# Score slots, direct plain heads and a merged ninth block in the attention half of a one-core kernel

## The chip, the core and the metric

The kernel runs on one NeuronCore of a Trainium2 chip. The core has five engines with instruction streams of their own: PE (TensorE: matrix products), DVE (VectorE) and ACT (ScalarE: elementwise work; both read the matmul results in PSUM), POOL (GpSimd: elementwise work on SBUF, and DMA issue) and SP (DMA issue only). Each engine runs its own stream strictly in order and waits on semaphores for the others. The metric is the device time of one execution in microseconds (us), as a median of runs.

## The reference, cut to what matters

```
# q, k, v: 8 batches x 8 heads x 576 rows x 64
scores = 0.125 * q @ k.T;  mask: heads 0-3 a plain band of 32 keys back,
                                  heads 4-7 every 4th key of 128 back
attn   = softmax(masked scores);  x = heads of (attn @ v) side by side    # 8 x 576 x 512
u      = x + real(fft(fft(x, axis=1), axis=2))
un     = (u - mean(u)) / sqrt(var(u) + 1e-6)
out    = u + relu(un @ w_ch1) @ w_ch2          # 512 -> 2048 -> 512
```

`w_ch1` and `w_ch2` arrive as 64-bit floats and are narrowed on the chip.

## The kernel before

The program is built by a planner. Each piece of work is an `add(engine, cost, function, reads, writes, priority)`; `Plan.run` simulates the engines with the costs written beside the pieces and, whenever an engine is free, gives it the ready piece of lowest priority number. The order that comes out is what each engine then executes; on the chip nothing but data dependences and buffer reuse holds a piece back. The constants at the top (`P_ST`, `P_W`, `NGANG`, ...) are offsets in those priorities, so changing them moves work on all engines.

**Attention.** A batch has 4 head pairs (2 plain, 2 dilated); a pair is cut into 2 units, so there are 64 units, 8 for each batch. `attend` makes one unit: 16 score matmuls (20 in a pair's second unit, which also holds the ninth block of 64 rows) of 64x96 into two PSUM banks; on DVE, for each 128x96 block, one custom instruction that masks, scales and takes the row maximum, with a second one that reads the maximum out (L663); on ACT one exponential for each block (L669); PE transposes (L683); an ACT copy to SBUF (L685, L689); value matmuls (L696); on DVE the row sum, its reciprocal and the multiplication (L706, L708, L709, L714) into `xt` and `xl`. The buffer "sc" is both score banks together, so the scores of one unit wait until the masks of the unit before have read them. The ninth block has its two heads in different banks and takes two 64-row mask instructions.

**Store and fold.** `store` writes a pair's rows to DRAM (`xsp`, `xsm`: rows folded in a forward and a mirrored half). Batch 0's plain heads go by DMA from `xt` (lent space in `ut`) straight into the `x` tiles in SBUF. `mix` folds the tiles (L853, L855, L867 to L877), multiplies them with DFT tables along the sequence (L904, L926) and along the channels (L950, L956), and adds. The constant `NFD = 1` puts the fold of batch 0 on DVE; other batches have it on POOL. The tables come by POOL's DMA queue, chained behind a one-element copy that reads `xt` of a chosen unit (`gone`, L581, L588).

**Fill.** `fill` is the first 6 of 16 column blocks of the feed-forward (L1080 up, L1096 down) on 256 tokens, put between attention work as soon as normalised rows and narrowed weights exist. `narrow` narrows a 64-bit block with ACT's absolute value (L1023) and four DVE steps (L1025, L1028, L1031, L1034); the last one zeroes what is below the 32-bit range. The remaining 10 column blocks (L1361, L1459, L1426) follow at the end.

**Warm-up matmuls.** `start` offers PE up to 250 pairs of matmuls on a zero tile (`blank`, L558) at the worst priority: the planner puts them wherever its simulation sees PE idle, until the first fill buffer ("ff") is taken. They are in the program for good: PE executes them in order even where work is ready behind them.

## Time and profile before

| what | value |
|---|---|
| time, median of 3 runs | 1022.49 us (1022.06 to 1023.35) |
| time of the profiled execution | 1022.32 us |
| its span in the profile | 1020.5 us |
| busy share PE, DVE, ACT, POOL | 99%, 74%, 47%, 29% |

The profile covers one execution. Its 1022.32 us hold the span of 1020.5 us, from the first to the last instruction, and 1.8 us around it. A busy PE counts warm-up matmuls too. By stretches: up to about 86 us the warm-up matmuls lie between attention work; from there to 552 us attention, mixing and fills share PE; from 552 us on PE runs the remaining column blocks.

### The profile page before, as it was taken

The page shows a single profiled execution, that of the slowest core. Times are in us where ns is not written, and L with a number is a line of the kernel's source. Part 1 is how long each engine was busy: PE and PEld are TensorE (multiplying, and loading weights), DVE is VectorE, ACT ScalarE, POOL GpSimd, SP SyncE. Part 2 cuts the span into 40 slices and gives each one's busy share as a digit, 9 for nine tenths or more (in the row PEclk, how much of TensorE's full clock was granted, in tenths as well). Part 3 has the DMA queues.
Part 4 walks back from the last instruction along what each step waited for, and adds up shares of the span by engine and source line. Part 5 has one row for each costly group of instructions (what it writes and reads, how often), then busy time and mean ns, then how long its engine had stood idle before and what let it go on. Part 6 is the DMA issues. An engine that isn't in the chain of part 4 may idle for free.

```text
span 1020.5 us, 22187 instructions
## 1 busy us (share of the span) xinstructions
PE 1006.4 (99%) x8347; PEld 898.2 (88%) x8347; DVE 750.4 (74%) x2203; ACT 479.4 (47%) x1186; POOL 291.4 (29%) x348
## 2 busy tenths in 40 slices
PE   9999999999999999999999999999999999999998
PEld 8788788888888888998988899999999989898987
DVE  4799967687867677686778876858585858585846
ACT  4776754464645444342445543535252525252522
POOL 2626454436243441846132510101010101010200
PEclk9999999999999999999999999999999999999999
DMA  9978765477656434432455232323232323232211
GB/s 313 305 240 252 220 199 175 146 209 212 197 151 195 120 118 135 150 105 93 132 169 155 84 83 83 84 83 83 83 84 83 83 84 83 83 84 83 83 62 42
DMA packets 99428, 138.49 MB, mean 136 GB/s; under 512 B 9838, under 2 KB 62619, under 8 KB 99321
## 3 DMA queue, kind: packets, MB, share of 16 engines
q1 hardware_dynamic: 94368, 126.10, 41.8%
q0 software_dynamic: 4032, 9.57, 3.2%
q8 instruction: 65, 1.06, 0.4%
q10 hardware_dynamic: 920, 1.41, 0.4%
q14 instruction: 43, 0.34, 0.1%
HBM read 99.24 MB, written 37.21 MB: 134 GB/s over the span
## 4 chain that ended last, share of the span: by engine, by line
PE 84%; DVE 8%; DMA 4%; issue 1%; ACT 1%; POOL 1%; ACTq 0%; SPq 0%; DVEq 0%; POOLq 0%
PE bank L1361 24%; PE bank L1459 20%; PE bank L1096 12%; PE bank L1080 11%; PE bank L950 3%; PE bank L696 3%; PE bank L683 3%; PE bank L632 2%; PE bank L558 2%; PE bank L904 2%; DMA ut<-in_w_dram 2%; PE bank L1426 1%; DVE pm L663 1%; DVE low L1088 1%; DMA ut<-us 1%
## 5 line engine op out<-in xcount | busy, mean ns | idle before, releaser
L1361 PE MATMUL bank<-low,wb 128*128 128x512 f32 x1080 | 255.9, 389 | 0.0
L1361 PEld LDWEIGHTS bank<-low,wb 128*128 128x128 f32 x1080 | 197.9, 188 | 37.4 <-ACT xb L1367 0.5
L1080 PE MATMUL bank<-ut,low 128*128 128x256 f32 x1296 | 168.0, 283 | 0.5 <-DVE low L1088 0.4
L1080 PEld LDWEIGHTS bank<-ut,low 128*128 128x128 f32 x1296 | 157.9, 189 | 3.7 <-DVE low L1088 1.5
L1096 PE MATMUL bank<-low 128*128 128x512 f32 x648 | 155.8, 393 | 0.0
L1124 POOL DMA_INDIRECT ut<-us,flip_sb x20 | 41.3, 2064 | 371.7 <-DVE ut L1181 243.1
L1096 PEld LDWEIGHTS bank<-low 128*128 128x128 f32 x648 | 118.7, 188 | 24.5 <-DVE low L1088 0.9
L1367 ACT ACTIVATE xa<-bank 128x256 f32<-128x256 f32 x90 | 34.2, 380 | 169.8 <-PE bank L1361 169.8
L669 ACT ACTIVATE pm<-pm,mx 128x96 f32<-128x96 f32 x256 | 83.7, 370 | 55.5 <-DVE mx L663 52.3
L1398 DVE TENSOR_TENSOR y<-xa 128x384 f32<-128x384 f32 x45 | 26.1, 581 | 95.5 <-ACT xa L1367 95.2
L1203 DVE STREAM_TRANSPOSE ut<-ut 128x512 f32<-128x512 f32 (+1 forms) x76 | 71.4, 977 | 11.4 <-DMA ut<-us 8.2
L1170 DVE TENSOR_TENSOR ut<-ut,bank 128x512 f32<-128x512 f32 (+1 forms) x136 | 73.1, 547 | 2.1
L1459 PEld LDWEIGHTS bank<-w2s,low 128*128 128x128 f32 x588 | 71.7, 188 | 2.1
L1459 PE MATMUL bank<-w2s,low 128*128 128x256 f32 x588 | 72.1, 278 | 0.0
L1086 ACT ACTIVATE low<-bank 128x256 fp32r<-128x256 f32 x108 | 41.2, 382 | 65.7 <-PE bank L1080 65.3
L1088 DVE SCALAR_TENSOR_TENSOR low<-bank,low 128x256 fp32r<-128x256 f32 x108 | 45.0, 419 | 31.4 <-ACT low L1086 30.5
L663 DVE CUSTOM_DVE_ANT_0 pm<-bank,mask_sb 128x96 f32<-128x96 f32 x256 | 55.5, 247 | 11.6 <-PE bank L632 10.4
L1459 PEld LDWEIGHTS bank<-w2s,hm 128*128 128x128 f32 x483 | 58.9, 188 | 1.8
L1459 PE MATMUL bank<-w2s,hm 128*128 128x256 f32 x483 | 59.2, 278 | 0.0
L1040 ACT CAST low<-y 128x640 fp32r<-128x640 f32 (+1 forms) x50 | 35.8, 717 | 40.0 <-DVE y L1400 24.8
L1116 ACT COPY row<-bank 128x512 f32<-128x512 f32 x36 | 21.0, 585 | 66.2 <-PE bank L1096 59.2
L1459 PE MATMUL bank<-low 128*128 128x256 f32 x420 | 51.5, 278 | 0.0
(182 smaller groups left out, 1833.5 us busy)
## 6 DMA issues: line engine op xcount, KB each, us to landing
qk<-in_qk_dram SPq DMA_DIRECT2D x30, 576.0 KB
vt<-in_v_dram SPq DMA_DIRECT2D x31, 438.8 KB
us<-uc SPq DMA_DIRECT2D x36, 257.0 KB
part<-row SPq DMA_DIRECT2D x36, 256.0 KB
wst<-in_w_dram SPq DMA_DIRECT2D x18, 512.0 KB
ut<-us SPq DMA_DIRECT2D x36, 256.0 KB
ut<-part SPq DMA_DIRECT2D x36, 256.0 KB
ut<-us SPq DMA_DIRECT2D x64, 128.0 KB
```

Source lines behind the costliest of these rows:

```text
L663: nc.vector.tensor_tensor_reduce(prob(i)[ps_], sc()[e][ps_, KB * (i // 2):KB * (i // 2) + KB], mask_sb()[ps_, kind], -0.125, 3.0e38, ALU.a ...
L669: add("ACT", 0.265, lambda i=i: nc.scalar.activation(out=prob(i), in_=prob(i), func=AF.Exp, bias=mx()[:, i:i + 1], scale=-1.0), ((mx, i),) ...
L1040: add("ACT", act(n), lambda: nc.scalar.copy(out=dst(0), in_=src()), need, ((key[0], (key[1], 0)),), prio)
L1080: nc.tensor.matmul(z()[:, :n_tok], lhsT=wf()[a][:, kk], rhs=ut()[:, p, kk], start=(kk == 0 and n == 0), stop=(kk == KT - 1 and n == 2),)
L1086: add("ACT", act(n_tok) - 0.05, lambda: nc.scalar.activation(out=h()[:, 0, :n_tok], in_=z()[:, :n_tok], func=AF.Relu), (z,), ((h, 0),), prio)
L1088: add("DVE", dve(n_tok), lambda: nc.vector.scalar_tensor_tensor(h()[:, 1, :n_tok], z()[:, :n_tok], 0.0, h()[:, 0, :n_tok].bitcast(F32), op ...
L1096: nc.tensor.matmul(acc(), lhsT=h()[:, a, P * s:P * s + P], rhs=wf()[:, p], start=(first and n == 0), stop=(last and n == 2),)
L1124: add("POOL", 1.04, lambda: nc.gpsimd.indirect_dma_start(dst(), None, us[idx // 4](), bass.IndirectOffsetOnAxis(ap=flip_sb()[:, 4 * kk + i ...
L1170: add("DVE", dve(C if at in (outer, inner) else TOK1), lambda: nc.vector.tensor_tensor(out=blocks(part())[:, at], in0=blocks(part())[:, at ...
L1203: nc.vector.transpose(out=o[back], in_=x[:, g])
L1361: nc.tensor.matmul(z(), lhsT=wb1[NF1 + 2 * p + f]()[:, a, kk], rhs=ut()[:, x, kk], start=(kk == 0 and n == 0), stop=(kk == KT - 1 and n == 2),
L1459: nc.tensor.matmul(acc()[block // 2][:, TOK1 * (block % 2):TOK1 * (block % 2) + TOK1], lhsT=part(hl, a, i, i + 1), rhs=w2s[p]()[:, j, x], ...
```

## The change

1. **Score slots.** A pair's first unit now uses columns 288 to 480 of both score banks ("scu"), the second unit columns 0 to 288 ("sc"); each has its own slot. Head and half are crossed (`e ^ h`), so that both heads of the ninth block lie in one bank and need one 128-row mask instruction instead of two of 64 rows. `NGANG` goes from 2 to 8: only from unit 8 on do scores also wait for the copy of the unit two before.
2. **Plain heads of batch 0.** Their last multiplication writes straight into the `x` tiles (4 instructions of 128 columns in a second unit, 2 in a first) instead of `xt` and a DMA; the second units ("straight") copy the probabilities into one long row with gaps and take 20 value matmuls instead of 10 (`across`).
3. **Narrowing.** The absolute value is clamped from below first (`max` with 2^-15, one source, in place of the compare-and-multiply of two sources at the end), and the first shift reads the clamped tile.
4. **Where work runs.** `NFD = 0`: the fold of batch 0 moves from DVE to POOL. Mask and identity come by POOL's DMA queue; the tables are plain POOL DMAs with planned times (`T_SEQ`, `T_CHN`) and no copy ahead of them. Batch 0's stores go by ACT and POOL in turn, its fold loads by ACT.
5. **Planner.** New costs for landing and mode switches, value matmuls as a mode of their own, new priorities and PSUM views (`NPT2`, `NAV2`).

```
-NPT2, NAV2 = 13, 16
-NGANG = 2
+NPT2, NAV2 = 16, 10
+NGANG = 8
-NFD, NUD = 1, 0
+NFD, NUD = 0, 0
-Q_ST0, Q_X0, Q_PL0 = "PPPP", "P", "AP"
+T_SEQ, T_CHN = 14.0, 38.0
+Q_ST0, Q_X0 = "AP", "A"
...
+    views = {"sc": [lambda: pair], "scu": [lambda: [t[:, 3 * KB:5 * KB] for t in pair]], ...
...
-        dma(lambda: nc.sync.dma_start(out=mask_sb(), in_=mask), (), (mask_sb,), -7.9, P * 5 * KB * 4)
+        add("POOL", 0.55, lambda: nc.gpsimd.dma_start(out=mask_sb(), in_=mask), (), (mask_sb,), -60.0, P * 5 * KB * 4)
...
+        direct = not b and not dil
+        straight = direct and u
-        sc = bank("sc")
+        sc = bank("sc" if u else "scu")
-                sc()[e][QB * h:QB * h + QB, KB * i:KB * i + KB], lhsT=...
+                sc()[e if straight else e ^ h][QB * h:QB * h + QB, KB * i:KB * i + KB], lhsT=...
-            for e in ((i % 2,) if i < 4 else range(2)):
+            for e in ((i % 2,) if i < 4 else range(2 if straight else 1)):
...
+        if direct:
+            for x, k, rows, to in (((xs[1], 0, ...), (xs[3], 2, ...), (xtail[1], 4, ...), (xtail[0], 4, ...)) if u else
+                                   ((xs[0], 0, ...), (xs[2], 2, ...))):
+                add("DVE", dve(P), lambda ...: nc.vector.tensor_tensor(out=x()[to, 0:C // 2]..., op=ALU.mult), ...)
+            return
...
+        add("DVE", 0.34, lambda: nc.vector.tensor_scalar(mag(), mag(), F64_LOW, None, op0=ALU.max), (), (m,), prio)
-            shaped(bits(U32)), words(1), 5, 2, op0=ALU.logical_shift_left, op1=ALU.logical_shift_right),
+            bits(U32), flat(t, 2 * C, C, U32), 5, 2, op0=ALU.logical_shift_left, op1=ALU.logical_shift_right),
-        add("DVE", 0.6, lambda: nc.vector.scalar_tensor_tensor(
-            bits(F32), mag(), F64_MIN, bits(F32), op0=ALU.is_ge, op1=ALU.mult), (m,), (v,), prio)
```

In the rows below `bank_135` and `bank_136` are the two score banks, `x2` counts a repeat. On PE at the very start, before the change (L558 warm-up, L632 scores of the first pair):

```order
L558 MATMUL bank_142<-blank 128x256 x34
L632 MATMUL bank_135<-qk_158 64x96
L632 MATMUL bank_136<-qk_158 64x96
L632 MATMUL bank_135<-qk_158 64x96
L632 MATMUL bank_136<-qk_158 64x96
L632 MATMUL bank_135<-qk_158 64x96
L632 MATMUL bank_136<-qk_158 64x96
L632 MATMUL bank_135<-qk_158 64x96
L632 MATMUL bank_136<-qk_158 64x96
L558 MATMUL bank_142<-blank 128x256 x8
L632 MATMUL bank_135<-qk_158 64x96
L632 MATMUL bank_136<-qk_158 64x96
```

The same place now (L562 warm-up, L634 scores, L685 transposes):

```order
L562 MATMUL bank_139<-blank 128x220 x46
L634 MATMUL bank_135<-qk_157 64x96
L634 MATMUL bank_136<-qk_157 64x96 x2
L634 MATMUL bank_135<-qk_157 64x96 x2
L634 MATMUL bank_136<-qk_157 64x96 x2
L634 MATMUL bank_135<-qk_157 64x96 x2
L634 MATMUL bank_136<-qk_157 64x96 x2
L634 MATMUL bank_135<-qk_157 64x96 x2
L634 MATMUL bank_136<-qk_157 64x96 x2
L634 MATMUL bank_135<-qk_157 64x96 x3
L562 MATMUL bank_139<-blank 128x220 x4
L685 MATMUL bank_137<-perm_sb,pm 96x128
```

Both units of the pair (18 matmuls) now stand together, behind 46 warm-up matmuls instead of 34. In both whole orders, 240 warm-up matmuls before and 216 now; the first fill matmul stands behind 19 units' value matmuls before and 17 now; when the last unit's value matmuls come, 633 up and 288 down matmuls have run before, 402 and 180 now; and from the first fill to the end of the fills PE changes 146 times between scores, values and all else before, 153 times now.

On SP, the loads at the start, before:

```order
L542 DMA mask_sb<-in_mask_dram 128x480
L543 DMA ident_sb<-in_ident_dram 128x384
L544 DMA perm_sb<-in_perm_dram 128x640
L617 DMA vt<-in_v_dram 96x1170 x3
L615 DMA qk_159<-in_qk_dram 128x1152
L617 DMA ut<-in_v_dram 96x1170
L615 DMA qk_160<-in_qk_dram 128x1152
```

and now:

```order
L548 DMA perm_sb<-in_perm_dram 128x640
L614 DMA qk_158<-in_qk_dram 128x1152
L614 DMA qk_159<-in_qk_dram 128x1152
L614 DMA ut<-in_qk_dram 128x1152
L616 DMA vt<-in_v_dram 96x1170 x3
L616 DMA ut<-in_v_dram 96x1170
L1040 DMA ut<-in_w_dram 128x4x128 x2
```

The keys and queries of all four pairs of batch 0 now stand ahead of every value tile; POOL's queue begins with mask, identity and the five sequence tables.

On ACT, around the end of batch 0's attention, before (L669 exponentials, L685 and L689 copies of probabilities, L537 loads into the `x` tiles):

```order
L685 COPY ptsb<-bank_137 96x512
L669 ACTIVATE pm<-pm,mx 128x96
L537 DMA xt_166<-ut 32x256
L537 DMA xt_167<-ut 32x256
L537 DMA x_163<-ut 63x256
L537 DMA x_163<-ut 64x128
L669 ACTIVATE pl<-pl,mx 128x96
L685 COPY ptsb<-bank_140 96x512
```

and now (L690 and L695 the copies, L541 loads from the stored rows, L1041 absolute values):

```order
L690 COPY ptsb<-bank_142 96x2x256
L1041 ACTIVATE ut<-ut 128x512
L541 DMA x_161<-xsp_59 128x256
L541 DMA x_163<-xsp_59 128x256
L541 DMA xt_165<-xsp_59 32x256
L541 DMA x_162<-xsm_67 128x256
L541 DMA x_164<-xsm_67 128x256
L541 DMA xt_166<-xsm_67 32x256
L541 DMA xt_165<-xsm_67 1x256
L541 DMA xt_166<-xsm_67 1x256
L695 COPY ptsb<-bank_141 96x2x64
```

Eight loads now stand in one block between the two copies of unit 7's probabilities; ACT issues 15 DMAs of this kind in all, 5 before.

## Rows read from the trace of the kernel before

**Rows 1.** The page: busy us, share of the span, instructions of each engine.

```profile
PE 1006.4 (99%) x8347; PEld 898.2 (88%) x8347; DVE 750.4 (74%) x2203; ACT 479.4 (47%) x1186; POOL 291.4 (29%) x348
```

**Rows 2.** Stretches: length, busy PE, PEld, DVE, ACT, POOL (instructions), clock, DMA share, GB/s.

```profile
8.30:40.00 31.70, 29.38 (x471) 25.26 (x471) 20.61 (x137) 20.49 (x61) 14.85 (x28) 1.00 1.05 322
40.00:140.00 100.00, 96.57 (x1261) 82.06 (x1254) 94.91 (x428) 68.78 (x194) 51.33 (x63) 1.00 0.80 241
140.00:200.00 60.00, 58.96 (x579) 52.00 (x578) 39.31 (x155) 26.28 (x71) 24.93 (x36) 1.00 0.55 164
200.00:372.00 172.00, 171.26 (x1886) 149.87 (x1885) 127.55 (x582) 92.71 (x263) 71.34 (x102) 1.00 0.58 174
552.00:1020.50 468.50, 464.30 (x2955) 420.30 (x2953) 332.56 (x617) 195.23 (x438) 53.97 (x31) 1.00 0.28 81
```

**Rows 3.** Timeline of the start: start, us, engine, line, count [idle before].

```profile
1.18 6.66 PE L558 MATMUL bank<-blank 128*128 128x256 f32 x34 [1.18 <-DVE blank L553]
...
7.77 0.56 PE L632 MATMUL bank<-qk 64*64 64x96 f32 x16
...
8.38 0.26 DVE L663 CUSTOM_DVE_ANT_0 pm<-bank,mask_sb 128x96 f32<-128x96 f32 x1 [5.21 <-PE bank L632]
...
8.56 0.25 DVE L663 CUSTOM_DVE_ANT_0 pm<-bank,mask_sb 128x96 f32<-128x96 f32 x1
```

**Rows 4.** What DVE waited for, 0 to 40 us: total, times, longest.

```profile
DVE pm L663 <- PE bank L632: 8.7, 5, 5.2
DVE sums L706 <- PE bank L696: 4.7, 5, 1.4
```

**Rows 5.** Groups of DVE instructions, 40 to 140 us: count, busy us, mean ns.

```profile
L1034 DVE SCALAR_TENSOR_TENSOR ut<-ut 128x512 f32<-128x512 f32 x10 | 7.4, 736 | 0.1
...
L1025 DVE TENSOR_SCALAR ut<-ut 128x512 uint32<-128x512 uint32 x10 | 6.2, 618 | 0.1
L663 DVE CUSTOM_DVE_ANT_0 pl<-bank,mask_sb 64x96 f32<-64x96 f32 x22 | 5.5, 251 | 0.3
```

**Rows 6.** The fold's first addition, all of it: ns min/median/max.

```profile
L853 POOL TENSOR_TENSOR t<-x,x x14: 727/738/1288, 91.9 to 433.2; 128x257 f32<-128x257 f32 x14
...
L853 DVE TENSOR_TENSOR t<-x,x x2: 418/420/423, 53.7 to 55.4; 128x257 f32<-128x257 f32 x2
```

**Rows 7.** The first narrowing step, all of it: ns min/median/max.

```profile
L1025 DVE TENSOR_SCALAR ut<-ut x14: 412/427/1514, 23.2 to 550.6; 128x512 uint32<-128x512 uint32 x14
```

**Rows 8.** Timeline at 109 us, POOL and DVE.

```profile
109.44 1.28 POOL L1042 TENSOR_TENSOR low<-ut,low 128x512 fp32r<-128x512 f32 x1 [1.34 <-ACT low L1040]
109.59 1.42 DVE L1025 TENSOR_SCALAR ut<-ut 128x512 uint32<-128x512 uint32 x1
```

**Rows 9.** Timeline of PE's weight loads, where fills and scores alternate.

```profile
89.14 0.42 PEld L1080 LDWEIGHTS bank<-ut,low 128*128 128x128 f32 x3
89.69 0.54 PEld L632 LDWEIGHTS bank<-qk 64*64 64x64 f32 x20
...
141.60 7.81 PEld L1080 LDWEIGHTS bank<-ut,low 128*128 128x128 f32 x66
149.34 8.02 PEld L1096 LDWEIGHTS bank<-low 128*128 128x128 f32 x36
```

**Rows 10.** Timeline at 39 to 43 us: ACT's queue and what follows it.

```profile
39.05 1.28 ACTq L537 DMA_DIRECT2D xt<-ut  x2
...
40.37 1.96 ACTq L537 DMA_DIRECT2D x<-ut  x2
...
42.38 0.38 ACT L669 ACTIVATE pl<-pl,mx 128x96 f32<-128x96 f32 x1 [3.32 <-DMA x<-ut]
...
42.81 0.32 PE L683 MATMUL bank<-ident_sb,pl 128*96 128x128 f32 x1 [1.06 <-ACT pl L669]
```

**Rows 11.** DMA issues, 10 to 60 us: KB each, median us to landing.

```profile
seq<-in_seq_dram POOLq DMA_DIRECT2D x4, 290.0 KB, 6.5
...
xsp<-xt POOLq DMA_DIRECT2D x4, 72.0 KB, 7.0
```

More of the change, by code (lines that the diff above doesn't have):

```diff
@@ L56 @@
 WIN = 32
-GAP = 64
+GAP = 32
 DIL = 4
@@ L421 @@
 SPIN = 900.0
-PIPE0, PIPE1, T_PIPE = 3.6e5, 2.7e5, 40.0
+LAND = {"SP": 1.6, "ACT": 1.6, "POOL": 2.8}
+PIPE0, PIPE1, T_PIPE = 3.2e5, 2.7e5, 55.0
 WINDOW = 4096 / 1200
-SWITCH = 0.18
+SWITCH = 0.09
 PLAIN_MASK = (1, 0, 0, 0)
@@ L644, in scores @@
                     score(e, NB - 1, e, 2)
-        op = add("PE", 0.1 * n, scores, (qk_,), (sc,), prio)
+        op = add("PE", C_S * n, scores, (qk_,), (sc, *hold), prio)
         op.mode = 1
@@ L690, in attend, with across @@
                 ((av, ("t", 4)),), ((pt, 1),), prio)
+        if straight:
+            add("POOL", 0.15, lambda: nc.gpsimd.memset(ends(0, 1), 0.0), (), ((pt, 2),), prio)
+            add("POOL", 0.15, lambda: nc.gpsimd.memset(pt()[:, 2 * ONE:PTW], 0.0), (), ((pt, 3),), prio)
+            add("DVE", 0.07, lambda: nc.vector.tensor_copy(out=ends(ONE - 1, 1), in_=ends(QB + 2 * P - 32, 1)), ((pt, 0),), ((pt, 4),), prio)
+        def across(e):
+            for k, g, lo, n, t in ((0, 0, 0, QB, 8), (0, 1, 64, QB, 7), (0, 1, 64, 1, 8), (2, 0, 128, QB, 6), (2, 0, 128, 1, 7),
+                                   (2, 1, 192, QB, 5), (2, 1, 192, 1, 6), (4, 0, 256, QB, 4), (4, 0, 256, 1, 5), (4, 1, 289, QB, 4)):
+                nc.tensor.matmul(
+                    av()[QB * g:QB * g + n, 65 * (k + e):65 * (k + e) + 65], lhsT=pt()[:, ONE * e + lo:ONE * e + lo + n],
+                    rhs=vt()[:, e, t], start=True, stop=True)
```

185 lines of the change are left out of this document (95 added, 90 removed), and 3 rows, old and new, of the table tiles.

## The prediction

> **What bounds the kernel now.** I began with the page's busy shares [rows 1]. PE at 99% looks like the answer, but its count holds warm-up matmuls, so the share says nothing of the stages in which these lie. The table by stretches is therefore read next [rows 2], and in it the reader should look for the engine that has least left beside PE. Up to 40 us nobody is full: DVE is busy 20.61 of 31.70 us and ACT 20.49, while the DMA share stands at 1.05. From 40 to 140 us DVE is busy 94.91 of 100 us, ACT 68.78 and POOL 51.33: DVE sets the pace there, and PE's 96.57 us are partly warm-up. From 140 to 372 us (60.00 and 172.00) PE is busy 58.96 and 171.26, DVE 39.31 and 127.55, that is two thirds to three quarters, so there PE's own stream is the time. From 552 us PE is busy 464.30 of 468.50 us; nothing of the change lies there, and I take those 468.5 us as fixed. The granted clock is 1.00 in every stretch shown, so no term of the sum is for the clock. What can be won is thus the idle time ahead of 40 us and DVE's work between 40 and 140 us; whatever leaves DVE after 140 us is worth nothing directly.
>
> Third come DVE's waits before 40 us [rows 4]: 8.7 us on score matmuls and 4.7 us on value matmuls, 13.4 in all. The longest, 5.2, is the wait for the first scores, which come at 7.77 us, right behind 34 warm-up matmuls that take from 1.18 to 7.84 [rows 3].
>
> **The change part by part.** The sum is made against the profiled execution, 1022.3 us (its span of 1020.5 and 1.8 around it), which is 0.2 below the median of 1022.49. A saving on DVE in the full stretch shortens it by the saving divided by DVE's busy share, 0.949, since the other 5% are waits that recur with the work.
>
> *Merged ninth block.* Ahead of 140 us 22 half masks [rows 5] become 11 whole ones. A 64-row mask lasts 0.251 us in the mean [rows 5], a 128-row mask 0.25 to 0.26 [rows 3]: halves cost what a whole costs. Two masks in a row start 0.18 us apart (8.38, 8.56) [rows 3], so one removed is worth 0.18 to 0.25. I take the pace: 11 x 0.18 = 2.0 us. The other merges lie before 40 us, among waits, or after 140 us, where DVE isn't the bound. The exponentials shrink alike, but ACT at 68.78 of 100 has room.
>
> *Fold of batch 0.* Twelve additions leave DVE. One takes 0.420 us there [rows 6], and the first two stand at 53.7 and 55.4 us, inside the full stretch: 12 x 0.42 = 5.0 us. On POOL one takes 0.738 [rows 6], 8.9 us in all, covered by POOL's 48.7 us without work in the same stretch [rows 2]. If that cover failed, the fold would end later and the first sequence products with it.
>
> *What POOL's work does to DVE.* At 109.44 us POOL starts an operation of two sources and is on it for 1.28 us; DVE's narrowing step of 109.59 takes 1.42 us [rows 8], where its median is 0.427 and its extreme 1.514 [rows 7]. A DVE operation on SBUF beside POOL can thus be stretched until POOL is done. Twelve more additions on POOL cost DVE between 0 and all of their 8.9 us. DVE's masks and divisions read PSUM, and the masks show no such stretching (0.251 in the mean of the busy stretch), so only a few of the twelve will meet narrowing or statistics: I take +1.0.
>
> The Trainium skill, page "SBUF — State Buffer", section "Who interferes with whom", states the strict form: the port pair that VectorE and GpSimd share is an exclusive lock, whoever comes first holds it for the whole instruction, and a VectorE instruction with two SBUF sources or in its two-port mode waits out a GpSimd one. It speaks against moving the fold. The row at 109 us agrees (1.42 beside 1.28, against 0.427 undisturbed). By this rule in its strictest reading, every addition meeting such an instruction, the term would be 8.9 in place of 1.0; that is the last rival below.
>
> *Narrowing.* The last step, 0.736 us in the mean of ten [rows 5], goes. A clamp of one source comes, an operation that the trace lacks; the nearest row is the one-source narrowing step, 0.618 in the mean in this stretch [rows 5] and 0.427 in the median [rows 7]. Ten tensors save 10 x 0.118 = 1.2 to 10 x 0.309 = 3.1 us; I take 2.1. The second bound supposes that the clamp isn't stretched by POOL.
>
> *DVE together:* 2.0 + 5.0 + 2.1 = 9.1 us, divided by 0.949 gives -9.6 us. The direct divisions add a few instructions of batch 0 before 40 us; their cover is DVE's 11.1 us without work there [rows 2].
>
> *More changes of mode on PE.* Three fill matmuls from 89.14 us on are followed by the next scores at 89.69 [rows 9]: 0.55 us. The pace within fills is (149.34 - 141.60) / 66 = 0.117 us [rows 9], so three should take 0.35. A change costs some 0.2 us. Seven more of them, 153 for 146: +1.4 us. If they fall where PE waits anyway they cost nothing, so the bounds are 0 and 1.4.
>
> *The start.* Forty-six warm-up matmuls of 220 columns stand ahead of the first scores, where 34 of 256 took 6.66 us [rows 3]. PE runs them even with the keys there: 6.66 x 46/34 x 220/256 = 7.74, so the first mask comes 1.1 us later. Against that, both units of a pair follow without waiting for each other's masks, which is what part of the 8.7 us of waits was. On the queues: the value tiles now stand on SP behind three more tiles of keys, and beside them run POOL's five tables, 290 KB each [rows 11]. At 322 GB/s [rows 2] these 1.45 MB are 4.5 us of transfer just where the DMA share is full, and value matmuls wait for what comes behind them. On ACT, four loads at 39.05 us held the queue for 1.28 + 1.96 us, and the exponential behind them had waited 3.32 us [rows 10], so one issue costs 0.8 us of ACT; ten more are 8 us against 11.2 us without work before 40 us [rows 2]. Between a gain of 4 us (a third of DVE's 13.4 us of waits) and a loss of 8 us (ACT's issues in full) I take +1.2, near the one part that has a row, the 1.1 of the warm-up.
>
> *No cost:* the 20 extra value matmuls run while warm-up matmuls still fill PE, and the absolute value, the clamp's place and the priorities leave the counts of the fills as they were.
>
> **Sum:** -9.6 + 1.0 + 1.4 + 1.2 = -6.0 us; 1022.3 - 6.0 = **1016.3 us**. With every bound at its best end (2.75 + 5.0 + 3.1 on DVE, nothing for POOL and modes, -4 at the start) it would be -15.4, with every one at its worst (8.2 on DVE, 8.9, 1.4, 8) +9.7; they will hardly all fall one way, and most of it lies in 1012 to 1020.
>
> **The rivals.** *Deeper gain, 1008 (1003 to 1012).* If the slots do at the start what they can, two thirds of DVE's 13.4 us of waits go, about 8 more. For it: units no longer wait for the other unit's masks. Against it: with the DMA share at 1.05 the waits may only pass from scores to tiles that haven't landed.
>
> *Nothing nets, 1022.* The saved time comes back after 140 us. Attention is packed closer: when the last unit's values come, 582 fill matmuls have run where it was 921, 339 fewer, worth 339 x 0.117 = 40 us of PE. DVE's 167 us of work from 140 to 372 us [rows 2] would have to fit some 192 us, 87% busy, near the 95% at which it sets the pace. Six us of new PE idle there, 3% of it, cancel the gain. Against it: PE waited under 2 us in those 232 us.
>
> *Slower, 1028: the eight loads at the head of ACT.* They read back stored rows and so wait for stores, whose transfers take 7.0 us from issue to landing [rows 11]. They stand in one block between two copies of unit 7's probabilities; the second copy, all exponentials behind it, and with them PE's transposes and values of the next unit wait. In the trace four loads without such a wait already left PE idle 1.06 us at 42.81 [rows 10]. Five us more of issuing and 7 of landing make up to 12 us; it decides from 6 us on, when the gain is used up, and at 12 the time is 1016.3 + 12 = 1028. Against it: the stores may have landed long before ACT comes there.
>
> *The port in full, 1024.2.* All twelve additions block DVE: 8.9 in place of 1.0, 1016.3 + 7.9. Against it: the masks' durations above.
>
> That the slots do nothing, because tiles are late, is in the forecast already: it takes no gain for them.
>
> **How the numbers follow.** The forecast has 0.48, the deeper gain 0.22, nothing nets 0.12, the blocked ACT queue 0.11, the full port 0.07. A measurement of this kernel can tell about 0.2% from no change, 2 us. Faster is the forecast and the deeper gain, 0.70; within 0.2% is "nothing nets" and half of the full port, whose price lies at that bound, 0.15; slower is the rest, 0.15. The range has to leave out no more than 0.2: from 1005, which cuts some 0.07 off the deeper gain, to 1026, which leaves out the blocked queue.
>
> **What the changed profile would show.** Right: first scores at about 8.8 us; no 64-row masks but in the two straight pairs; DVE's busy time per unit down, the first fill before 86 us, the late stage beginning near 546 rather than 552 and lasting 468 us again. Each step has its place: the clamp's mean should lie between 0.43 and 0.62 us, the fold on POOL near 0.74, and DVE's two-source narrowing steps no longer than now. Wrong: an ACT wait of over 6 us ahead of unit 8's exponentials with PE idle behind it; DVE waiting on tiles of values or on sequence tables before 40 us for more than 13.4 us; PE idle for more than 2 us between 140 us and the end of attention. A late stage of another length would overturn the assumption that nothing changes behind 552 us.

## The result: 11 us slower, and the loss lies between 25 and 61 us

The changed kernel takes 1033.7 us (1033.5 to 1035.6) where the kernel before takes 1022.3 in the same runs: a ratio of 1.011, 95% interval 1.0092 to 1.0129. The forecast was 1016.3 us, the range 1005 to 1026. The profiled execution of the changed kernel is the slowest of its four (1035.6 us, a span of 1033.8), so its trace holds some 2 us more than the median does.

The page's busy times, to hold against [rows 1], and its lines of PE's busy tenths and of the granted clock in 40 slices:

```profile
PE 1010.6 (98%) x8363; PEld 898.8 (87%) x8363; DVE 729.7 (71%) x2139; ACT 475.5 (46%) x1186; POOL 286.3 (28%) x344
...
PE   9698999999999999999999999999999999999998
...
PEclk9699999999999999999999999999999999999999
```

PE is still busy 98%. The slice in which it lost something is the second, with a 6 for its busy time and a 6 for its clock. The table by stretches of the changed kernel is read as in [rows 2]: length, busy time (instructions) of PE, PEld, DVE, ACT and POOL, granted clock, DMA share, GB/s.

```profile
8.30:40.00 31.70, 21.44 (x337) 17.60 (x335) 11.24 (x95) 14.31 (x46) 3.42 (x8) 0.84 1.03 288
27.80:37.30 9.50, 0.04 (x1) 0.02 (x1) 1.53 (x13) 0.98 (x3) 0.00 (x0) 0.61 0.84 261
37.30:46.90 9.60, 9.59 (x55) 6.60 (x55) 2.91 (x10) 4.29 (x12) 0.15 (x2) 0.50 0.36 106
40.00:140.00 100.00, 94.98 (x1176) 78.03 (x1176) 80.89 (x362) 62.81 (x177) 45.93 (x58) 0.95 0.66 197
...
565.00:1033.80 468.80, 464.48 (x2957) 420.75 (x2955) 320.82 (x603) 192.40 (x435) 44.66 (x25) 1.00 0.27 78
```

Against [rows 2], the last line is untouched: 468.8 us for 468.5. The first shows the damage: DVE is busy 11.24 us where it was 20.61, PE 21.44 where it was 29.38. For 9.5 us PE does nothing at all, and the 9.6 us behind that run at a granted clock of 0.50, the lower level (1.2 GHz). The same two places in the rows by line, first of the kernel before, then of the changed one (first and last start of a kind of weight load): the first fill (L1080, now L1097) and the late stage (L1361, now L1379).

```profile
L1080 PEld LDWEIGHTS bank<-ut,low x1296: 186/188/233, 86.3 to 544.7; 128*128 128x128 f32 x186
...
L1361 PEld LDWEIGHTS bank<-low,wb x1080: 186/188/189, 551.6 to 994.6; 128*128 128x128 f32 x180
```

```profile
L1097 PEld LDWEIGHTS bank<-ut,low x1296: 186/188/233, 101.3 to 556.9; 128*128 128x128 f32 x186
...
L1379 PEld LDWEIGHTS bank<-low,wb x1080: 187/188/188, 565.0 to 1007.7; 128*128 128x128 f32 x180
```

In these traces the first fill is 15.0 us late and the late stage 13.4, so the whole loss is there before the first fill; 1.6 us come back in between.

What holds PE at 28 us stands in the timeline of ACT's queue (start, us, engine, line, [idle before <- releaser]; ACTq is a transfer that ACT issues):

```profile
22.59 0.58 ACT L690 COPY ptsb<-bank 96x512 f32<-96x512 f32 x1
26.61 0.56 ACTq L541 DMA_DIRECT2D xsp<-xt  x1
28.19 2.02 ACTq L541 DMA_DIRECT2D xsm<-xt  x2
30.26 0.58 ACT L690 COPY ptsb<-bank 96x512 f32<-96x512 f32 x1 [7.09 <-DMA qk<-in_qk_dram]
32.42 2.35 ACTq L541 DMA_DIRECT2D xsm<-xt  x2
35.90 0.31 ACTq L541 DMA_DIRECT2D xsp<-xt  x1
36.30 0.51 ACTq L541 DMA_DIRECT2D xsm<-xl  x1
36.91 0.26 ACT L695 COPY ptsb<-bank 96x128 f32<-96x128 f32 x1 [6.06 <-DMA xsm<-xt]
```

and PE's own, at the same time and at the second straight unit:

```profile
25.15 2.69 PE L562 MATMUL bank<-blank 128*128 128x220 f32 x22
37.31 6.42 PE L707 MATMUL bank<-vt,ptsb 96*64 96x65 f32 x40 [9.47 <-ACT ptsb L695]
...
52.83 4.16 PE L707 MATMUL bank<-ut,ptsb 96*64 96x65 f32 x40
```

From 23.2 to 36.9 us ACT did one copy of 0.58 us. The rest is seven stores of batch 0 that it issues in between, each waiting. The profile names a load of keys as what the first ones waited for, though a store reads nothing of the keys. The built program says why. It lists for each transfer what it waits for; these are ACT's first three stores, and the loads early in SP's queue that had the same counters (DMAHW1 to DMAHW3) before them:

```
L541 DMA xsp_59<-xt 72x256 [waits DMAHW1_49,DVE_49]
L541 DMA xsm_67<-xt 16x256 [waits DMAHW2_49]
L541 DMA xsm_67<-xt 40x256 [waits DMAHW3_49]

L1040 DMA ut<-in_w_dram 128x4x128 [waits DMAHW1_49]
L1040 DMA ut<-in_w_dram 128x4x128 [waits DMAHW2_49]
L614 DMA qk_157<-in_qk_dram 128x1152 [waits DMAHW3_49,PE_49]
```

In this program every transfer that SP or ACT issues takes one of eight counters in turn, one turn for both queues together, and it waits until the transfer that had its counter last has landed. ACT's stores thus wait for two loads of weights (512 KB each) and a prefetch of keys that SP had put into full DMA queues. The planner keeps eight places for SP and another eight for ACT (`lanes`), and so put the stores where it expected no wait. So more than data dependences and buffer reuse holds a piece back on the chip: a counter shared with another engine's queue does too.

A second suspect is in PE's timeline: a straight unit's value matmuls take 4.16 us at 52.83, and 6.42 at the lower clock.

### The profile page after: what moved, and what is told of

It reads as the page before. It is cut to its first block, busy times and chain, and to the rows that moved or that the text cites. A ratio compares the mean times of both kernels' runs of the same rounds, so it can differ in the third digit from the quotient of the medians.

```text
span 1033.8 us, 22185 instructions
## 1 busy us (share of the span) xinstructions
PE 1010.6 (98%) x8363; PEld 898.8 (87%) x8363; DVE 729.7 (71%) x2139; ACT 475.5 (46%) x1186; POOL 286.3 (28%) x344
## 4 chain that ended last, share of the span: by engine, by line
PE 89%; DVE 4%; DMA 2%; ACT 2%; issue 1%; POOL 1%; SPq 0%; DVEq 0%; POOLq 0%; ACTq 0%
PE bank L1379 24%; PE bank L1477 20%; PE bank L1113 13%; PE bank L1097 13%; PE bank L968 3%; PE bank L685 3%; PE bank L721 3%; PE bank L634 3%; PE bank L922 2%; PE bank L562 2%; PE bank L1444 1%; DMA qk<-in_qk_dram 1%; PE bank L707 1%; DMA ut<-us 1%; ACT pm L671 1%
## 5 line engine op out<-in xcount | busy, mean ns | idle before, releaser
L1379 PE MATMUL bank<-low,wb 128*128 128x512 f32 x1080 | 255.6, 389 | 0.0
L1379 PEld LDWEIGHTS bank<-low,wb 128*128 128x128 f32 x1080 | 198.0, 188 | 37.0
L1097 PE MATMUL bank<-ut,low 128*128 128x256 f32 x1296 | 166.4, 282 | 0.0
L1097 PEld LDWEIGHTS bank<-ut,low 128*128 128x128 f32 x1296 | 156.8, 188 | 2.5
L1113 PEld LDWEIGHTS bank<-low 128*128 128x128 f32 x648 | 118.3, 188 | 23.2 <-POOL low L1059 0.2
L671 ACT ACTIVATE pm<-pm,mx 128x96 f32<-128x96 f32 x256 | 81.2, 369 | 36.9 <-DVE mx L665 36.3
L665 DVE CUSTOM_DVE_ANT_0 pm<-bank,mask_sb 128x96 f32<-128x96 f32 x256 | 53.4, 248 | 19.7 <-PE bank L634 16.9
L690 ACT COPY ptsb<-bank 96x512 f32<-96x512 f32 x64 | 36.9, 578 | 35.0 <-PE bank L685 27.0
```

What stands on the lines that cost most here:

```text
L665: nc.vector.tensor_tensor_reduce(prob(i)[ps_], sc()[e][ps_, KB * (i // 2):KB * (i // 2) + KB], mask_sb().bitcast(F32)[ps_, kind], -0.125, ...
L671: add("ACT", 0.265, lambda i=i: nc.scalar.activation(out=prob(i), in_=prob(i), func=AF.Exp, bias=mx()[:, i:i + 1], scale=-1.0), ((mx, i),) ...
L690: op = add("ACT", act(4 * P) - 0.05, lambda: nc.scalar.copy(out=ends(QB + 1, 2 * P) if straight else pt()[:, 0:4 * P], in_=ps()[:KB, :4 * ...
L1097: nc.tensor.matmul(z()[:, :n_tok], lhsT=wf()[a][:, kk], rhs=ut()[:, p, kk], start=(kk == 0 and n == 0), stop=(kk == KT - 1 and n == 2),)
L1113: nc.tensor.matmul(acc(), lhsT=h()[:, a, P * s:P * s + P], rhs=wf()[:, p], start=(first and n == 0), stop=(last and n == 2),)
L1379: nc.tensor.matmul(z(), lhsT=wb1[NF1 + 2 * p + f]()[:, a, kk], rhs=ut()[:, x, kk], start=(kk == 0 and n == 0), stop=(kk == KT - 1 and n == 2),
```

## Experiments

All ratios are to the kernel before in the same runs, with 95% intervals. Its median in these runs lies between 1022.4 and 1023.6 us, so the ratios compare better than the times.

### The two suspects, and the tables

In e1_pool the edit is one word; e2_wide changes the order within `across`; e3_both has both.

```
-        ... "A": (nc.scalar, "ACT", 0.5)}[b]
+        ... "A": (nc.gpsimd, "ACT", 0.5)}[b]
```

> The changed kernel with one edit: the DMAs of batch 0 that ACT issues (7 stores, 8 fold loads) are issued by POOL at the same place of the program. Theory A (ACT's own queue: its stores wait, between copies of probabilities, for the landing of earlier transfers that SP issued; PE then stands idle 9.5 us from 27.8 us and its granted clock falls to 0.50): the idle piece at 27 to 37 us and the half clock behind it go, unit 6 (sixth) has its row sums near 33 us instead of 43.8, and the time falls by 8 to 13 us to 1021 to 1026. Rival B (the transfers are late because the tables fill the DMA queues at the start): the same matmuls wait as long for something else, 1031 to 1035. Rival C (the value matmuls with one column of weights, 4.1 us for one unit at full clock): at most the half-clock part goes, 1028 to 1031.

Measured: 1021.1 us, ratio 0.9992 (0.9978 to 1.0007), some 12 us below the changed kernel. The first fill stands at 86.8 us. Theory A holds: the idle piece and the lower clock are gone (1.00 throughout). Its stretch from 40 to 140 us and its first fill:

```profile
40.00:140.00 100.00, 94.94 (x1250) 78.14 (x1251) 86.94 (x388) 67.14 (x187) 57.39 (x71) 1.00 0.76 224
...
L1097 PEld LDWEIGHTS bank<-ut,low x1296: 186/188/233, 86.8 to 541.2; 128*128 128x128 f32 x186
```

PE has the same order in both kernels, so that each of its instructions can be compared with itself in the two traces. At 26 us the changed kernel is 0.4 us ahead of e1_pool, at 37.3 us 9.1 behind, at 47.0 12.9 and at 62.6 14.5; from there to 140 us nothing is added, and by the late stage 1.1 us. Of the 14.9 us, 9.5 are thus PE's idle piece, 3.8 the lower clock behind it and 1.6 a second piece at the lower clock (57 to 61 us).

The value matmuls of the first straight unit, now at the full clock, run from 28.2 to 32.1 us, still 4 us:

```profile
L707 PEld LDWEIGHTS bank<-vt,ptsb x40: 79/133/138, 28.2 to 32.1; 96*64 96x64 f32 x24, 96*1 96x1 f32 x16
```

```
-        def across(e):
-            for k, g, lo, n, t in ((0, 0, 0, QB, 8), (0, 1, 64, QB, 7), (0, 1, 64, 1, 8), ...
-                nc.tensor.matmul(
+        def across(wide):
+            for e in range(2):
+                for k, g, lo, n, t in ((0, 0, 0, QB, 8), (0, 1, 64, QB, 7), (0, 1, 64, 1, 8), ...
+                    if (n > 1) == wide:
+                        nc.tensor.matmul(
...
-                across(0)
-                across(1)
+                across(True)
+                across(False)
```

> The changed kernel with one edit: in the two straight units the 12 value matmuls of 64 columns of weights run first and the 8 of one column after them, instead of alternating. Rival C (each change between wide and narrow costs 0.2 us): a straight unit's value matmuls take 1.0 to 1.5 us at full clock instead of 4.1, and the time falls by 4 to 7 us to 1027 to 1030. Theory A alone: the stall of 9.5 us ahead of them stays, and of the 3 us saved at each unit at most 3 in all arrive at the end, 1030.5 to 1033.5. Rival B: 1033 to 1034.

Measured: 1025.3 us, 1.0025 (1.0011 to 1.0038), 8.7 us below the changed kernel and below every expectation. The two straight units in this run, in the first of which the clock is at the lower level:

```profile
L709 PEld LDWEIGHTS bank<-vt,ptsb x40: 79/226/231, 36.1 to 38.2; 96*64 96x64 f32 x24, 96*1 96x1 f32 x16
...
L709 PEld LDWEIGHTS bank<-ut,ptsb x40: 79/136/138, 46.8 to 48.0; 96*64 96x64 f32 x24, 96*1 96x1 f32 x16
```

Between the first and the last of the 40 loads lie 1.2 us at the full clock, where e1_pool has 3.9, and 2.1 at the lower one, where the changed kernel has 6.0. In the alternating order wide and narrow change 16 times in a unit, here once: (3.9 - 1.2) / 15 is 0.18 us a change. A narrow matmul also rewrites a row that the wide one ahead of it has just written, but that isn't what it waits for: in e1_pool's trace the loads start 0.20 us apart at every change, from wide to narrow and from narrow to wide alike, and at most 0.06 apart within a kind. ACT's stall is still there (PE waits 8.4 us), so this gain is rival C's: 2.7 and 3.9 us at the two units, 1.1 from a stall of 8.4 us for 9.5, and 1.0 that the ratios don't assign. In the two traces, where the first fill comes 10.3 us earlier (91.0 us), the changed kernel's second piece at the lower clock is missing as well, which is worth 1.6.

> Both edits together (POOL issues what ACT issued for batch 0; wide value matmuls first). If A and C are both causes and independent: their gains add, 1015 to 1021, below the kernel before. If C was only visible because PE waited anyway: the same as the first edit alone within 1.5 us. Rival B: 1030 or above.

Measured: 1022.9 us, 0.9997 (0.9984 to 1.0011). The gains do not add: 12 and 8.7 us together give 11.6. A new idle piece of PE stands at 43 us. It shows in DVE's waits between 40 and 60 us,

```profile
DVE ee L887 <- POOL t L875: 5.2, 1, 5.2
```

in POOL's timeline,

```profile
39.22 1.11 POOL L541 DMA_DIRECT2D x<-xsp  x2 [5.79 <-DMA xsp<-xt]
...
45.11 0.72 POOL L873 TENSOR_TENSOR t<-x,x 128x257 f32<-128x257 f32 x1 [1.54 <-DMA x<-xsm]
```

and in PE's:

```profile
47.75 0.45 PE L685 MATMUL bank<-ident_sb,pm 128*96 128x128 f32 x1 [4.90 <-ACT pm L671]
```

PE now arrives before batch 0's rows have been to DRAM and back. Stores wait for landing, loads for stores, POOL's fold for loads; a DVE addition of the fold, which needs POOL's, has masks behind it in its queue, and exponentials wait for those.

```
-            add("POOL", 0.55, lambda: nc.gpsimd.dma_start(out=dst(), in_=src), (), (key,), prio, ...)
+            go = lambda: nc.gpsimd.dma_start(out=dst(), in_=src)
+            add("POOL", 0.55, (lambda: held.append(go)) if prio == P_SEQ else go, (), (key,), prio, ...)
...
+                if sent[0] == 6:
+                    for t in held:
+                        t()
```

> The changed kernel with one edit: the five sequence tables leave POOL's queue behind the first six stores of batch 0 (about 27 us) instead of at 2.8 us; 1.45 MB less to move before 25 us. Rival B (tables crowd the transfers that the stores wait for): the stall from 27.8 to 37.3 us is gone or under 3 us and the time is 1022 to 1027. Theory A: the stores still wait for SP's transfers, which land up to 4.5 us earlier; the stall shrinks to 5 to 8 us and the time to 1028 to 1032. Rival C: 1032 to 1034.

Measured: 1028.6 us, 1.0055 (1.0038 to 1.0073). ACT's copies wait 4.7 us for stores instead of 7.1 + 6.1, and PE 2.2 instead of 9.5. The clock falls all the same, to 0.50 from 30.7 to 40.9 us, and the value matmuls behind take 6.27 us. The stall is as short as rival B has it, the time as long as theory A has it. So the tables make the waits for counters long; they are not what ACT waits for.

### Stores or loads

```
-Q_ST0, Q_X0 = "AP", "A"
+Q_ST0, Q_X0 = "QP", "A"
...
+        ... "Q": (nc.gpsimd, "ACT", 0.5)}[b]
```

> The changed kernel, of whose 15 transfers on ACT only the 7 stores are issued by POOL; the 8 fold loads stay on ACT. If the stores make the loss (in the trace ACT's copy of probabilities stands behind them until 36.9 us, and PE idle until 37.3): 1021 to 1024, as with all 15 on POOL (1021.1). If the eight loads make it, as the prediction's rival had it: 1030 to 1034. If the wait only moves from the stores to the loads, which need the stored rows: 1025 to 1030, with ACT held at the loads for over 5 us.

Measured: 1027.1 us, 1.0049 (1.0034 to 1.0064): the third case. The wait moves to the eight loads, in ACT's waits from 20 to 70 us:

```profile
ACT ptsb L695 <- DMA xt<-xsm: 8.7, 1, 8.7
```

PE waits 2.8 us, the clock is at 0.50 twice (31.7 to 35.1 and 45.3 to 52.2 us), and the first fill comes at 93.4 us, between 101.3 and 86.8. In the changed kernel the stores make the loss, and the copy behind the loads waits only 2.9 us; without the stores the loads hold ACT as the rival of the prediction had it.

### What DVE's time is worth

These two take the kernel before, keep its order, and change only DVE's load.

```
-                sc()[e][QB * h:QB * h + QB, ...
+                sc()[e ^ h][QB * h:QB * h + QB, ...
...
+                    if i == 4 and e:
+                        return
...
-        add("DVE", 0.6, lambda: nc.vector.scalar_tensor_tensor(bits(F32), mag(), F64_MIN, ...), (m,), (v,), prio)
+        add("DVE", 0.6, lambda: None, (m,), (v,), prio)
```

> The kernel before in its own order, with less work on DVE and nothing else moved: the ninth block's two half masks merged into one (heads and halves crossed in the two score banks) and the last narrowing step left out (what lies below the 32-bit range is not zeroed). From 40 to 140 us that takes 11 x 0.18 + 10 x 0.736 = 9.4 us off DVE, as much as the 9.1 us of the prediction's sum. Theory D (DVE sets the pace from 40 to 140 us, as the prediction has it): 7 to 10 us faster, 1012.5 to 1015.5. Rival E (what sets the pace there is PE's own order, its warm-up matmuls included, and chains between engines; DVE is full because work waits in its queue): DVE's busy time in the stretch falls to about 86 us, the time by 0 to 3 us, 1019.5 to 1022.5.

Measured: 1018.3 us, 0.9947 (0.9926 to 0.9968), 5.4 us faster by the ratio, between the two. Its stretches, and then those of the kernel before:

```profile
40.00:88.00 48.00, 47.07 (x649) 41.67 (x649) 41.11 (x191) 32.13 (x91) 25.85 (x36) 1.00 0.92 273
88.00:140.00 52.00, 50.96 (x661) 42.95 (x664) 47.41 (x212) 37.48 (x107) 29.15 (x33) 1.00 0.76 229
```

```profile
40.00:88.00 48.00, 46.81 (x649) 41.26 (x642) 43.78 (x202) 32.08 (x90) 23.97 (x32) 1.00 0.90 272
88.00:140.00 52.00, 49.76 (x614) 40.80 (x614) 51.13 (x227) 36.70 (x104) 27.36 (x31) 1.00 0.71 213
```

The stretch of 100 us that the prediction took as one is two. From 88 us DVE is busy 51.13 of 52 us in the kernel before; ahead of that it is busy 43.78 of 48. PE's order is the same in both kernels here too, and its instructions show where the time goes in these two traces. At 33.5 us b1_dve is 1.8 us late: PE waited 3.4 us up to 27 us instead of 1.5, DVE ahead of it 3.8 us for a load of weights instead of 1.9, and the clock stood at 0.50 from 28.0 to 31.4. At the first fill it is 1.6 us late (88.0 for 86.3), so from there on the work taken off DVE bought 0.2 us. From 88 to 139 us it gains 2.9, and from there to the late stage (548.0 for 551.6) another 2.4, most of it between 376 and 450 us, where the same step was left out of other weights. So DVE sets much of the pace from 88 to 140 us, hardly any of it before, and some of it later, where the prediction put nothing.

```
-        on = nc.vector if dve_ else nc.gpsimd
+        on = nc.gpsimd
```

> The kernel before in its own order, with the 12 additions of batch 0's fold on POOL instead of DVE at the same places. Prediction's own terms: DVE loses 12 x 0.42 = 5.0 us, POOL's blocking gives back 1.0: 4 us faster, 1018.3. Rival E: DVE's time isn't the pace, and the fold is a chain of batch 0 (0.738 instead of 0.420 each, with SBUF operations of DVE stretched meanwhile): 0 to 4 us slower, 1022.5 to 1026.5, with the first sequence product later than 56.05 us.

Measured: 1025.1 us, 1.0016 (0.9999 to 1.0034). DVE's busy time from 40 to 140 us falls from 94.91 to 88.61, and the time doesn't: the group of the fold's next addition (xcount | busy, mean ns | idle before)

```profile
L867 DVE TENSOR_TENSOR ee<-t,t 128x257 f32<-128x257 f32 x4 | 1.7, 419 | 3.7 <-POOL t L855 3.7
...
L867 DVE TENSOR_TENSOR ee<-t,t 33x257 f32<-33x257 f32 x2 | 0.8, 423 | 2.3 <-POOL t L855 2.3
```

waits 6.0 us for POOL. Moving five microseconds off DVE put six of waiting on it. By PE's instructions the loss arises with the fold and its products: b2_fold is 0.4 us ahead at 42 us and 2.5 behind at 64 us and at the first fill (88.8 for 86.3). That the first product itself would come later did not show (55.7 us for 56.0).

### What holds PE ahead of 88 us

The chain of work that ended last in that stretch, followed back, holds many warm-up matmuls. Half of those behind 40 us were taken out, from b1_dve and from the repaired kernel (e6_tables, below).

```
+                turns[0] += 1
-                for _ in range(2):
+                for _ in range(2 if turns[0] <= 59 else 1):
```

> The kernel with less DVE work in the order before (merged ninth block, last narrowing step left out), and half of the warm-up matmuls that stand behind 40 us taken out (61 of 122). If they hold PE between 40 and 88 us: the first fill comes 2 to 6 us before 88.0 us and the time falls by as much, 1012.5 to 1016.5. If the chain of batch 0 (stores, loads, fold, products) sets that stretch: first fill at 87 to 88 us, 1017.5 to 1019.5. If PE idles enough for its granted clock to fall: slower, above 1020, with the clock under 1.00 between 40 and 88 us.

Measured: 1017.3 us, 0.9948 (0.9929 to 0.9967): as b1_dve (0.9947). The first fill comes at 88.5 us. In this trace PE is 2.3 us behind b1_dve before the edit takes effect (at 40 us, with the clock at 0.50 from 28.2 to 35.0) and 0.9 at 88 us: it makes up 1.4 us on the way.

> The changed kernel with both repairs and the tables behind the stores, and half of the warm-up matmuls behind 40 us taken out (36 of 72). If they hold PE: first fill 1 to 4 us before 85.5 us, 1016 to 1019. If the chain of batch 0 does: no difference to 1020.2 within 1 us. If the clock falls: above 1021.5.

Measured: 1020.2 us, 0.9985 (0.9969 to 1.0001), e6_tables being at 0.9972: no gain. Here the clock did fall, with PE busy 41.67 of the 48 us:

```profile
40.00:88.00 48.00, 41.67 (x510) 34.16 (x510) 40.63 (x167) 31.49 (x87) 31.91 (x41) 0.86 0.73 212
```

and the first fill moved from 85.5 only to 87.0. PE is 1.4 us ahead of e6_tables at 77 us; then the clock is at 0.50 from 76.8 to 87.0, and it comes to the first fill 1.6 behind. So half of the warm-up matmuls hold PE by some 1.4 us in either kernel, and no more, and the time shows none of it. That the chain of batch 0, from its stores to its first normalised rows, sets the rest is likely but not shown: the lower clock lies over both tests.

### Repairs

e5_plan lets the planner know of the shared counters, of 1.45 us for a straight unit's value matmuls, and sends stores and loads by POOL.

```
+        lanes["ACT"] = lanes["SP"]
-        op = add("PE", 0.122 * (n + 5 * straight), values, ...)
+        op = add("PE", 1.45 if straight else 0.122 * n, values, ...)
-Q_ST0, Q_X0 = "AP", "A"
+Q_ST0, Q_X0 = "P", "P"
```

> The changed kernel planned anew with what the runs showed: transfers issued by SP and by ACT share one set of eight slots in the planner, the straight units' value matmuls stand wide first and are costed at 1.45 us (1.22 before), batch 0's stores and fold loads go by POOL (Q_ST0 = Q_X0 = P). All priorities are unchanged. If the two causes found (ACT's queue, narrow weights) are all that stood between the change and its forecast: no stall over 3 us of PE before 90 us, granted clock 1.00 throughout, 1014 to 1019. Rival E: the stalls go, and the time still comes out near that of the kernel before, 1020 to 1025, because a shorter DVE buys nothing while PE runs its planned order.

Measured: 1032.8 us, 1.0089 (1.0067 to 1.0111). A new order with old priorities is a new kernel: between 40 and 60 us DVE waits 4.3 us for POOL's fold, whose loads land after 48 us, and the first fill comes at 98 us. Neither of the two signs came: PE waits 3.9 us at 56.8, and the clock falls to 0.50 three times between 57 and 153 us. It says nothing of the two causes; the edits that keep the order do.

e6_tables starts from e3_both and holds the tables back as e4_tables does, counting all stores of batch 0:

```
-                if sent[0] == 6:
+                if sent[0] == 13:
```

> Both repairs of the changed kernel (POOL issues what ACT issued, wide value matmuls first) and, besides, the five sequence tables leave POOL's queue behind batch 0's thirteen stores (about 33 us) instead of at 2.8 us. In the run with both repairs PE stood idle 4.9 us at 43 us: exponentials wait behind the fold, the fold for loads of rows whose stores landed 6 us after their issue. If the full DMA queues make that chain late: the idle piece goes or falls under 2 us, 1016 to 1019.5. If it is the chain's own length (issue, landing, issue, landing): it stays, and the tables now land behind it, 1022 to 1026.

Measured: 1020.2 us, 0.9972 (0.9958 to 0.9986): faster than both kernels, and the lowest ratio among the versions of the changed kernel, though its interval overlaps that of e1_pool. b1_dve and b4_turns, which leave a narrowing step out of the kernel before, are lower still (0.9947, 0.9948). The idle piece is gone as expected: the longest wait of PE between 30 and 60 us is 1.2 us, and the first fill stands at 85.5 us. The time lies 0.7 us above the range that was tied to it.

e7_fold is e3_both, and e8_all is e6_tables, with batch 0's fold executed on DVE where the planner has it on POOL:

```
-            either(b < NFD, NEH, lambda on: on.tensor_tensor(
+            either(b < 1, NEH, lambda on: on.tensor_tensor(
...
-        add("DVE" if dve_ else "POOL", (dve if dve_ else pool)(n), lambda: go(on), r, w, prio)
+        was = dve_ and NFD
+        add("DVE" if was else "POOL", (dve if was else pool)(n), lambda: go(on), r, w, prio)
```

> Both repairs, and batch 0's fold on DVE at the same places of the order instead of on POOL (as the kernel before has it). By the fold moved alone in the kernel before (1.6 us slower on POOL): 1 to 3 us faster than with both repairs, 1019.5 to 1022. By the prediction's terms (5.0 us of DVE time, 1.0 us of blocking): 4 us slower, 1027. If the idle piece at 43 us comes from loads that land late, it stays in either case, and DVE waits there itself.

Measured: 1025.4 us, 1.0014 (0.9997 to 1.0031), no faster than e3_both: DVE itself now waits 5.4 us for the loads (`t<-x,x` for `x<-xsm`).

> Both repairs, the tables behind the stores and the fold on DVE. If late landings and the fold on POOL are what the repaired kernel still lacks: 1013 to 1018, clearly below the kernel before. If the gains of the single edits again take each other's place, as with the first two repairs: 1019 to 1024.

Measured: 1021.4 us, 0.9988 (0.9967 to 1.0008): not separable from e6_tables. A difference by the engine of the fold can't be told here.

b3_best puts two parts of the change into the order before: merged ninth block and clamp.

```
+        def low_then_shift():
+            absolute()
+            nc.vector.tensor_scalar(mag(), mag(), 2.0 ** -15, None, op0=ALU.max)
...
-        add("DVE", 0.34, lambda: nc.vector.tensor_scalar(shaped(bits(U32)), words(1), 5, 2, ...), src, (v,), prio)
+        add("DVE", 0.34, low_then_shift, src, (v,), prio)
```

> The kernel before in its own order with two parts of the change alone: the ninth block's two half masks merged, and the weights clamped from below first in place of the last narrowing step. DVE loses 2.0 + 10 x (0.736 - 0.43 to 0.62) = 3.2 to 5.1 us between 40 and 140 us. By what the run with 9.4 us less on DVE gave (5.2 us at the end, since only from 88 us on does DVE set the pace): 2 to 3 us faster, 1020 to 1021.5 where the kernel before has 1023. If every microsecond of DVE counted: 3.4 to 5.4 us faster. If none: no difference.

Measured: 1031.5 us, 1.0082 (1.0062 to 1.0102), a miss. The old first shift read the loaded words; the clamp reads ACT's absolute value, and in this order that comes late (DVE's waits from 8 to 140 us, then from 140 to 552):

```profile
DVE ut L1036 <- ACT ut L1032: 6.2, 4, 2.3
...
DVE wst L1036 <- ACT wst L1032: 10.0, 6, 2.8
```

So the clamp trades a DVE instruction for a dependence on ACT, which the changed kernel's order has more room for (DVE waits 8.1 us for it in its whole run) than the order before. PE is 5.2 us behind the kernel before at the first fill, 4.4 at 370 us and 9.0 at the late stage: the loss has an early part and one behind 370 us, where the second of these waits lies. Of the early part 3.5 us are there by 30 us, with a wait of 2.1 us for keys among them; how the rest divides was not traced.

## Why the prediction was wrong

Two steps failed above all. *The start* priced ACT's added transfers by what issuing takes, 0.8 us each against ACT's idle time, and took +1.2 us for the whole step. In the runs ACT was held for 13 us by what the transfers wait for; PE stood idle for 9.5 us and lost 5.4 more at the lower clock, and with these transfers on POOL 12 us come back. *DVE together* put -9.6 us on DVE's work; with that loss taken away, the whole change stands at -0.8 us. The steps in their order:

*What bounds the kernel.* Half right. The late stage was fixed (468.8 for 468.5). That no term is for the clock was wrong: it is 0.95 from 40 to 140 us in the changed kernel, and was at 0.50 from 57.1 to 60.5 us although PE had work. The view that misled was one stretch from 40 to 140 us with a share of 95%. Cut at the first fill it shows a half in which DVE is full and one in which work taken off DVE bought 0.2 us. Of 9.4 us off DVE in that stretch 5.4 arrived (b1_dve), where the step's divisor of 0.949 would have made 9.9; and some of the 5.4 arose behind 140 us.

*Merge and clamp.* The sizes held. The clamp takes 0.562 us in the changed kernel, inside the bounds of 0.43 to 0.62, for the 0.736 of [rows 5]:

```profile
L1050 DVE SCALAR_TENSOR_TENSOR ut<-ut 128x512 uint32<-128x512 uint32 x10 | 8.8, 883 | 0.1
...
L1043 DVE TENSOR_SCALAR ut<-ut 128x512 f32<-128x512 f32 x10 | 5.6, 562 | 0.1
...
L885 DVE TENSOR_TENSOR ee<-t,t 128x257 f32<-128x257 f32 x4 | 3.4, 858 | 0.0
...
L887 DVE TENSOR_TENSOR oo<-t,t 32x256 f32<-32x256 f32 x2 | 1.8, 904 | 0.1
```

DVE's busy time from 40 to 140 us is 86.94 in e1_pool, 8.0 below the 94.91 of before, where 9.1 less 1.0 was forecast (the stretch holds nearly, not exactly, the same work). Right in size, and wrong in what it is worth.

*Fold on POOL.* This step gained nothing. It priced the time that DVE saves (5.0 us) and the port (1.0), and took POOL's idle time as cover. It did not ask who in DVE's queue waits for POOL's result: the fold's own next addition, with masks behind it. Moved alone it cost 1.6 us (-0.1 to +3.5, b2_fold) instead of gaining 4.0; the interval leaves open whether it costs anything, and excludes the gain.

*The port.* The mean of four additions `ee` went from 0.415 to 0.858 us and that of two `oo` from 0.417 to 0.904, but not beside the moved additions. Lines of the kernel before, of b2_fold (both 40 to 140 us), and of the changed kernel's timeline:

```profile
L867 DVE TENSOR_TENSOR ee<-t,t 128x257 f32<-128x257 f32 x4 | 1.7, 415 | 0.0
```

```profile
L1025 DVE TENSOR_SCALAR ut<-ut 128x512 uint32<-128x512 uint32 x10 | 6.7, 665 | 0.1
```

```profile
66.51 1.28 POOL L1059 TENSOR_TENSOR low<-ut,low 128x512 fp32r<-128x512 f32 x1
...
66.56 1.52 DVE L885 TENSOR_TENSOR ee<-t,t 128x257 f32<-128x257 f32 x1
```

Three single additions make these means: 1.52, 1.07 and 1.39 us. Each runs beside L1059, a subtraction for the weights that both kernels have on POOL, and two of the three are of batch 1, whose fold was on POOL before. In b2_fold, where the fold alone moves, `ee` keeps 0.419, and of the narrowing steps only the first grows, 0.618 to 0.665 us: ten times 0.047, or 0.5 us, where 1.0 was taken and the rival had 8.9. In the changed kernel the narrowing steps moved both ways (L1028 1.025 to 0.847, L1031 0.774 to 0.883). The Trainium skill, page "SBUF — State Buffer", section "Who interferes with whom", says that of VectorE and GpSimd whoever comes first holds the shared port pair for the whole instruction; the row at 66.5 us agrees, with 1.52 us for an addition that started 0.05 us behind POOL's.

*The start.* The first scores come at 8.69 us (8.8 forecast). What the step priced wrongly is ACT's issues: 0.8 us each, as [rows 10] had it, against idle time. The price was not in the issuing (the eight loads took 3.4 us of it, 0.4 each) but in what an issue waits for, 13 us of ACT between 23.2 and 36.9. The 12 us that e1_pool gives back lie outside the step's bounds of -4 and +8. It also read the tables too small: [rows 11] has four of 290 KB, and the fifth has 435, so they are 1.6 MB and not 1.45.

*No cost for the extra value matmuls.* Failed twice. The cover named was warm-up work, but PE executes that in any case, so what comes on top is on its path. And a price was missing for narrow weights between wide ones: 2.7 us more for each of the two straight units than with the narrow ones put last. The Trainium skill, page "TensorEngine Tiling (Array Packing)", section "Key Properties", says that a change of tiling mode, not of the tile alone, drains TensorE. The profile names forms (96*64 and 96*1) and not modes; 0.18 us for each change of form, in both directions, agrees with it.

*The modes.* Not tested by themselves. From first fill to late stage the changed kernel needs 463.7 us, the one before 465.3, with other work among the fills.

*The rivals.* The right one was named, ACT's queue held by transfers, with 0.11; it was put at the eight loads, where seven stores come first, and its price at 12 us above the forecast, where 17.4 came. Its sign, ACT waits of over 6 us with PE idle behind them, came (7.09 and 6.06 us), at unit 5 and not ahead of unit 8. It lacked the counters shared with SP and the halved clock after the idle piece. "Nothing nets" has e1_pool's time: with the stores and loads off ACT the change stands at 0.9992 of the kernel before. It doesn't have its mechanism, for from 140 to 372 us PE is idle 1.5 us there and 1.8 before, where the rival had six more. With the measured terms, merge and clamp 4.1 x 5.4 / 9.4 = 2.4 us of gain and the fold 1.6 of loss, the sum is -0.8 us, and e1_pool is at -0.8 (-2.2 to +0.7). That agreement is no proof: it leaves out the start and the modes, it prices the clamp at b1_dve's rate although the only run of merge and clamp alone (b3_best) was 8 us slower, and the fold's 1.6 isn't clear of zero.

What stays open: whether batch 0's chain sets the first fill, and by which of its later steps, once stores and loads are in time (e6_tables to e10_turns all have it at 85 to 87 us or behind), what lets the clock fall while PE is busy, and the early part of b3_best's loss.

## What to carry to other kernels

A transfer issued from a computing engine can block that engine for as long as transfers of other engines take, here ACT for 13 us: before putting one into ACT's queue, look up what its wait is on, not what the issue costs. When work leaves the busiest engine, ask which instruction in that engine's queue needs the result; if it is the next one, the saved time can come back as a wait. And cut a stretch at the events of the program (first fill, last unit) before calling an engine its bound.
